# Batch 0's v tails through the SyncE and ScalarE queues with a VectorE cast, and a new order of work

## The chip, the cores and the metric

The kernel runs on one core of a Trainium2 chip. The metric is the device time of one execution in microseconds. The kernel before takes 288.69 us (median of 3 runs, 288.6 to 288.89). The program's span in its profile is 287.0 us.

## The reference

Two blocks follow one another. The first is attention with random features (Performer) over 8 batches of 8 heads, 576 positions, head size 64, 128 features. The second is an MLP mixer over tokens (576 to 256 to 576) and channels (512 to 1536 to 512). Inputs and outputs are fp32.

```python
batch, n_heads, seq, head_dim = (8, 8, 576, 64)
def phi(x):
    proj = np.einsum('bhsd,md->bhsm', x, omega)
    sq = np.sum(x * x, axis=-1, keepdims=True) / 2.0
    h = proj - sq
    h = h - np.max(h, axis=-1, keepdims=True)
    return np.exp(h) / np.sqrt(m)
q_p, k_p = (phi(q_s), phi(k_s))          # q, k times 1 / sqrt(sqrt(64))
kv = np.einsum('bhsm,bhsd->bhmd', k_p, v)
z = np.sum(k_p, axis=2)
num = np.einsum('bhsm,bhmd->bhsd', q_p, kv)
den = np.einsum('bhsm,bhm->bhs', q_p, z)[..., None] + 1e-06
x = num / den                             # then heads side by side: (8, 576, 512)
h = np.maximum(x.T @ w_tok1, 0.0) @ w_tok2     # x.T: per batch, channels by tokens
u = x + h.T
out = u + np.maximum(u @ w_ch1, 0.0) @ w_ch2
```

## The kernel before

**Tiling.** The 576 positions of a batch are 512 "main" positions and a "tail" of 64. Main positions fill 128 partitions four times. The tails of the eight heads are packed together. All matmuls have fp16 operands, so nearly every load casts fp32 to fp16 on its way. Such loads are issued by Pool. The exceptions are batch 0's k (main), which is loaded as fp32 by the SyncE and ScalarE queues into `first_k` and transposed as fp32, and omega.

**Stages of one batch.** Batches 0 and 1 have q and k loaded by position and transposed by TensorE (L485 main, L505 tails). Later batches have them cast to a scratch in DRAM by Pool and transposed by a DMA from the SyncE queue. Then come, for each pair of heads (`hp`): k projection `kp` (L638) and its exp on ScalarE (L514); VectorE's maximum `km` (L664) and its reciprocal (L666); Pool's scaling of v, `vs` (L671); the product `kv` (L684, with the tails' part at L691 or L693); a copy `kvsb` (L701); q projection (L652) and exp; the numerator (L720, L722); and the division into `x` (L729, L730). The tails of k go through one projection per batch (L546, "kt") and exp, the tails of q through L611. The tails of v are loaded by `load_v_tail` into `t_vt` (two loads of four heads each) and spread by Pool into the block-diagonal operand `vbd` (L565 for batch 0 after VectorE's maximum L552, L596 for the others). Every kv product needs `vbd`.

The token mix of batch 0 works by 128 channels (`token_mix_first`: "t1" at L803 and L804, "ut" at L819 and L821); for later batches it is L759, L760 and L776. The channel mix is L854 (first half; L860 and L862 for batch 0's first two blocks) and L892 (second half). The tails of two batches share one token tail (L835), and all tails go through a ninth channel mix at the end. The result is added on VectorE and stored.

**What sets the order.** The program is written down by a planner. Each piece of work is a `Job` with an engine, an assumed cost, a key, dependencies and places (buffers). `Planner.run` steps through assumed time: for the engine that can go first it takes, among the jobs that are ready, the one with the lowest key. The keys of batches 1 and up come from `KEYS` and `NEAR`, those of batch 0 from `HEAD`. For loads the planner keeps an assumed wire time and adds `AFTER`; a product that waits for a load gets an extra margin. Engines then run their instructions in the written order. So assumed costs and keys decide the order, and true times decide the waits. Up to eight loads of a queue are outstanding (`LANES`): the ninth waits for the first.

While batch 0 is under way and TensorE would stand idle by the plan, the planner inserts products on zeros (L943, `warm`). They compute nothing that is used; they end at the first channel mix (L860).

The Pool loads keep the order in which the program lists them (`job.after`). The list before begins:

```python
load_nat_tail(0, "k", -8.7)
load_v_tail(0, -8.65)
load_nat(0, "q", 0, 4, -8.6)
load_v(0, -8.55, (), 0, 4)
load_nat(0, "q", 4, 8, -8.5)
load_nat_tail(0, "q", -8.48)
load_v(0, -8.45, (), 4, 8)
```

then the token weights, the first half of `w_ch1`, and batch 1's k, v tails, q and v.

Of the kernel before, what the change touches and what calls it, by code (L numbers as in the profile page):

```python
# [13 lines left out]
AX = mybir.AxisListType  # L14


KEYS = {"a": -1.349, "as": 0.099, "t": -1.509, "ts": 0.187, "gv": 2.165, "lt": -2.428, "lv": -3.989, "to": -2.341, "tt": 0.635, "ks": 1.094, "km": 0.303, "vs": -0.113, "l1": -0.452, "kt": -0.062}
NEAR = {"1": {"a": -1.734, "as": 0.259, "t": -2.775, "ts": 0.45, "gv": -0.056, "km": -2.03, "vs": -0.397, "kt": 0.253}, "2": {"a": -2.686, "as": 0.0, "t": -0.603, "ts": 0.324, "gv": -1.313, "km": 3.931, "vs": 0.571, "lv": -3.347, "lt": -2.872, "kt": -0.122}}
HEAD = {"kp": [-3.838, -3.822, -3.881, -3.404], "ke": [-2.728, -2.927, -2.827, -2.727], "km": [-4.039, -3.592, -4.221, -2.25], "vs": [-3.448, -3.487, -3.196, -2.472], "qp": [-3.203, -3.403, -3.303, -3.488], "qe": [-3.328, -3.374, -2.153, -3.748], "kv": [-3.407, -3.257, -2.676, -3.133], "ko": [-2.32, -3.035, -3.463, -3.168], "n": [-3.199, -3.47, -3.182, -2.377, -2.999, -3.268, -2.999, -2.899], "no": [-4.124, -3.487, -3.919, -3.144, -3.226, -3.426, -3.126, -2.386], "ktm": -3.643, "kt": -4.584, "kte": -5.022, "qt": -3.759, "qte": -5.587, "kx": [-6.213, -5.658, -5.326, -5.458], "kxo": [-6.855, -7.05, -5.723, -4.783], "ktx": -5.661, "ktxo": -5.912, "qx": [-4.987, -3.488], "qxo": [-4.073, -2.977], "qtx": -4.584, "qtxo": -3.371, "t1": [0.229, -1.008, -0.737, -0.359], "re": [0.072, -0.781, 0.181, -0.024], "ut": [0.056, -0.48, -0.104, -0.341], "uo": [-0.099, -0.259, -0.108, 0.38], "vbd": -8.41, "w1": -9.7, "w1t": -9.38, "w2t": -9.78, "wa": -8.03, "wb": -9.17, "w2": -10.08}
# [18 lines left out]
class Planner:  # L38
# [5 lines left out]
    MARGIN = {"PE": 0.3, "ACT": 0.05, "DVE": 0.05, "POOL": 0.05, "SP": 0.0}  # L44
    LANES = 8
    BEFORE = {"POOL": 1.5, "SP": 0.8, "ACT": 0.8}
    AFTER = 0.8
    SWITCH = 0.1
    COLD = 5.5

# [25 lines left out]
    def run(self):  # L76
# [6 lines left out]
        while any(waiting.values()):  # L83
            choice = None
            for eng, jobs in waiting.items():
                ready = []
                for j in jobs:
                    t = at[eng]
                    ok = True
                    if j.after is not None and j.after.end is None:  # L90
                        continue
                    for d in j.deps:
                        if d.end is None:
                            ok = False
                            break
                        m = self.MARGIN[eng] if d.eng != eng else (-self.LATENCY["PE"] if eng == "PE" else 0.0)
                        if eng == "PE" and self.warm is not None:
                            m = min(m, 0.05)
                        if eng == "PE" and d.wire:
                            m = 0.5  # L100
                        t = max(t, d.end + m)
                    if not ok:
                        continue
                    self.now = t
                    got = []
                    for tag, name in j.take:
# [24 lines left out]
            eng = j.eng  # L131
            waiting[eng].remove(j)
            if self.warm is not None and eng == "PE":
                if j.heavy:
                    self.warm = None
                else:
                    while t - at["PE"] > 0.3:
                        self.now = at["PE"] + 0.1
                        free = [i for i, at_ in enumerate(self.places["bank"]) if at_ < self.now]
                        if free:  # L140
                            i = min(free, key=lambda i: (self.warmed.get(i, 0), i))
                            self.warmed[i] = self.warmed.get(i, 0) + 1
                            self.warm(i)
                            last_rows = False
                        at["PE"] += 0.43 if at["PE"] < self.COLD else 0.22
                    t = max(t, at["PE"])
            self.now = t
            for tag, name in j.take:
                if (tag, name) not in self.held:
                    i = self.find(tag)[0]  # L150
                    self.places[tag][i] = math.inf
                    self.held[tag, name] = i
            cost = j.cost
            if eng == "PE":
                cost += self.SWITCH if j.rows != last_rows else 0.0
                last_rows = j.rows
            at[eng] = t + cost
            if j.wire:
                wire = max(wire, t + cost + self.BEFORE[eng]) + j.wire
                j.end = wire + self.AFTER  # L160
                lanes[eng].append(j.end)
            else:
                j.end = t + cost + self.LATENCY[eng]
            j.start = t
            j.fn()
            for g in j.give:
# [11 lines left out]
def kernel(  # L178
# [12 lines left out]
    nc = tc.nc  # L191

    B, H, S, D = q.shape
# [4 lines left out]
    P = 128  # L198
    SM = 512
# [9 lines left out]
    NPE = 2  # L209
# [15 lines left out]
    place = plan.place  # L225
# [12 lines left out]
    w1t = sb([P, 2, DT], FP16, "w1t")  # L238
    w2 = sb([P, NT, S], FP16, "w2")
# [69 lines left out]
    ld = {}  # L309
# [26 lines left out]
    def load_v_tail(b, key, deps=()):  # L336
        jobs = []
        for g in range(2):
            def tails(g=g):
# [3 lines left out]
                    o = t_vt[place("vt", b)][g * ST : (g + 1) * ST].rearrange("p a (c d) -> p (a c) d", c=2)  # L343
                    i = v[b, :, SM:S, :].rearrange("(a i) t d -> i t a d", i=2)[g]
                nc.gpsimd.dma_start(out=o, in_=i)
# [92 lines left out]
    j_w2 = dma("POOL", HEAD["w2"], 1.7, lambda: nc.gpsimd.dma_start(out=w2, in_=moe_w_tok2.rearrange("(i p) s -> p i s", p=P)))  # L438
    def w2_of(tb, j):
        return w2[:, tb, 0:SM].rearrange("p (c j) -> p j c", j=NJ)[:, j, :]  # L440
    j_wc1 = []
    def load_wc1(i):
        c0 = i * (DC // 2)
        j_wc1.append(dma("POOL", HEAD[("wa", "wb")[i]], (3.9, 4.4)[i], lambda: nc.gpsimd.dma_start(
            out=wc1[:, :, c0 : c0 + DC // 2], in_=moe_w_ch1[:, c0 : c0 + DC // 2].rearrange("(i p) c -> p i c", p=P))))
    load_wc1(0)
    load_nat(1, "k", 0, 8, -9.61)
# [528 lines left out]
```

The softmax here doesn't subtract the row's maximum and nothing guards it: scores larger than these inputs give would overflow.

## Time and profile before

| | before |
|---|---|
| time | 288.69 us |
| span of the profile | 287.0 us |
| PE busy | 280.2 us, 98% |
| PE weight loads busy | 141.6 us, 49% |
| VectorE busy | 152.6 us, 53% |
| ScalarE busy | 153.6 us, 54% |
| Pool busy | 93.7 us, 33% |
| channel mix, L892 and L854 | 100.7 us and 88.7 us of PE |
| Pool's first loads issued | k tails 1.44 us, v tails 2.22 us, q 3.67 us |

PE is TensorE's matmuls, PEld its weight loads, DVE VectorE, ACT ScalarE, SP SyncE. A q after an engine's name is its queue of issued loads. Times in a timeline are microseconds from the start of the span, first the start and then the duration. In brackets stands the idle time of that engine before the instruction, and what ended it. A line of the waits view has the total, the number of times and the longest. Matmuls overlap, so their printed durations are longer than their spacing: a product of 512 columns is printed as 379 ns, and eight of them follow one another in 1.73 us.

### The profile page before, as it was taken

Reading aid. Unit: us, or ns where it says so; the run is one execution under the profiler, and the core shown is the slowest. Engines: PE = TensorE matmul, PEld = TensorE weight load, DVE = VectorE, ACT = ScalarE, POOL = GpSimd, SP = SyncE. Lnnn points to the kernel's source line nnn. Section 1 sums busy time; section 2 is a strip of 40 time slices with the busy share of each in tenths; the row PEclk is TensorE's granted clock in tenths of the full one; section 3 lists DMA queues with packets and bytes.
Section 4 is the critical chain, followed back from the end, with each engine's and each line's share of the span. In section 5 each row is a group of like instructions: output and inputs, shape, how many; then the busy total and the mean of one; then the engine's idle time right before and its main releaser. Section 6 shows DMA issues by size and latency. Waiting matters only on the chain.

```text
span 287.0 us, 5605 instructions
## 1 busy us (share of the span) xinstructions
PE 280.2 (98%) x2186; PEld 141.6 (49%) x2186; DVE 152.6 (53%) x330; ACT 153.6 (54%) x322; POOL 93.7 (33%) x126
## 2 busy tenths in 40 slices
PE   8999999999999999999999999999999999999994
PEld 4585554445544544454445544454455444444442
DVE  3986954546669624745584647564686331031012
ACT  2984872098449552875286537753576402602600
POOL 8994950157015701480166016601141000000000
PEclk9999999999999999999999999999999999999999
DMA  8999999999975995999989967996531042013013
GB/s 191 197 191 195 202 216 143 214 196 190 166 110 149 136 175 117 202 168 198 111 156 206 201 85 144 199 189 95 129 75 39 0 110 110 2 48 116 2 45 102
DMA packets 85721, 39.59 MB, mean 138 GB/s; under 512 B 64384, under 2 KB 80128, under 8 KB 85504
## 3 DMA queue, kind: packets, MB, share of 16 engines
q0 software_dynamic: 34288, 17.45, 44.4%
q1 hardware_dynamic: 50624, 21.01, 33.2%
q10 hardware_dynamic: 784, 0.79, 0.8%
q8 instruction: 17, 0.28, 0.4%
q14 instruction: 8, 0.07, 0.1%
HBM read 35.88 MB, written 16.52 MB: 183 GB/s over the span
## 4 chain that ended last, share of the span: by engine, by line
PE 90%; POOL 5%; DMA 3%; issue 1%; ACT 0%; DVE 0%; POOLq 0%; DVEq 0%
PE bank L892 33%; PE bank L854 32%; PE bank L776 4%; PE bank L759 4%; DMA r<-in_k_dram 3%; PE bank L638 3%; PE bank L652 3%; PE bank L684 2%; PE bank L720 2%; POOL vs L671 1%; PE bank L760 1%; POOL r L313 1%; PE bank L835 1%; PE bank L485 1%; PE bank L722 1%
## 5 line engine op out<-in xcount | busy, mean ns | idle before, releaser
L892 PE MATMUL bank<-wc,r 128*128 128x512 f16 (+2 forms) x444 | 100.7, 374 | 0.0
L874 ACT ACTIVATE r<-bank 128x512 f16<-128x512 f32 x106 | 62.7, 606 | 64.5 <-PE bank L854 64.4
L854 PE MATMUL bank<-uT,wc 128*128 128x512 f16 x376 | 88.7, 379 | 0.0
L892 PEld LDWEIGHTS <-r 128*128 128x128 f16 x444 | 40.9, 98 | 48.9 <-issue 4.4
L854 PEld LDWEIGHTS <-wc 128*128 128x128 f16 x424 | 39.7, 98 | 43.1 <-issue 0.4
L514 ACT ACTIVATE qp<-bank 128x512 f16<-128x512 f32 x64 | 35.8, 646 | 13.0 <-PE bank L652 13.0
L664 DVE TENSOR_REDUCE km<-kp 128x8 f16<-128x1024 f16 x32 | 38.5, 1202 | 2.3 <-ACT kp L514 2.3
L514 ACT ACTIVATE kp<-bank 128x512 f16<-128x512 f32 x64 | 34.6, 630 | 6.6 <-PE bank L638 6.4
L671 POOL TENSOR_TENSOR vs<-v,vs 128x512 f16<-128x512 f16 x32 | 33.3, 1063 | 13.8 <-DVE vs L666 4.3
L901 DVE TENSOR_TENSOR o<-u,bank 128x512 f32<-128x512 f16 x28 | 19.1, 683 | 34.5 <-PE bank L892 34.4
L730 DVE TENSOR_TENSOR x<-bank,rc 128x320 f16<-128x320 f32 x62 | 30.5, 492 | 2.1
L779 DVE TENSOR_TENSOR u<-x,bank 128x512 f16<-128x512 f16 x28 | 17.4, 683 | 9.5 <-PE bank L776 9.5
L729 DVE RECIPROCAL rc<-bank 128x5 f32<-128x5 f32 x62 | 11.5, 186 | 16.0 <-PE bank L722 15.8
L596 POOL TENSOR_TENSOR vbd<-vt,vbd 128x512 f16<-128x512 f16 (+1 forms) x7 | 8.2, 1173 | 35.0 <-PE bank L835 14.8
L380 POOL COPY junk<-kT 128x1 f16<-128x1 f16 x6 | 1.1, 186 | 50.5 <-DMA kT<-k 50.5
L767 DVE TENSOR_SCALAR r<-bank 128x512 f16<-128x512 f32 x7 | 4.8, 692 | 21.1 <-PE bank L760 21.1
L759 PE MATMUL bank<-x,w1m 128*128 128x512 f16 x56 | 14.4, 379 | 0.0
L720 PEld LDWEIGHTS <-qp 128*128 128x128 f16 x256 | 12.3, 98 | 4.0
L684 PEld LDWEIGHTS <-kp 128*128 128x128 f16 x256 | 11.1, 98 | 5.7 <-issue 1.1
L684 PE MATMUL bank<-vs,kp 128*128 128x65 f16 x256 | 12.9, 194 | 0.7 <-ACT r L874 0.7
L720 PE MATMUL bank<-kvsb,qp 128*128 128x65 f16 x256 | 13.5, 194 | 0.0
L776 PE MATMUL bank<-r,w 128*128 128x512 f16 x56 | 13.4, 380 | 0.0
(109 smaller groups left out, 269.5 us busy)
## 6 DMA issues: line engine op xcount, KB each, us to landing
out_dram<-o SPq DMA_DIRECT2D x32, 256.0 KB, 2.7
q<-in_q_dram POOLq DMA_DIRECT2D x6, 576.0 KB, 6.8
wc<-in_moe_w_ch_dram POOLq DMA_DIRECT2D x4, 768.0 KB, 10.6
k<-in_k_dram POOLq DMA_DIRECT2D x6, 512.0 KB, 9.1
v<-in_v_dram POOLq DMA_DIRECT2D x6, 512.0 KB, 6.7
r<-in_q_dram POOLq DMA_DIRECT2D x4, 256.0 KB, 7.2
v<-in_v_dram POOLq DMA_DIRECT2D x4, 256.0 KB, 7.1
out_dram<-o SPq DMA_DIRECT2D x5, 128.0 KB, 2.3
```

The source lines that it names most:

```text
L514: nc.scalar.activation(out=out, in_=in_, func=AF.Exp, bias=0.0, scale=1.0)
L664: nc.vector.reduce_max(out=mx, in_=kpv, axis=AX.X)
L671: nc.gpsimd.tensor_tensor(out=vs[:, :, 0:D], in0=t_v[place("v", b)][:, hh[0] : hh[0] + 2, :].rearrange("p h (j d) -> p (h j) d", d=D), in1 ...
L684: nc.tensor.matmul(ps[:, i, :], kpv[:, 2 * i + j // 2, j % 2, :], vs[:, i * NJ + j, 0 : D + 1], start=(i == 0 and j == 0), stop=False, ski ...
L720: nc.tensor.matmul(ps[:, k, j * 65 : (j + 1) * 65], st, s[:, i, 0 : D + 1], start=True, stop=True)
L730: nc.vector.tensor_tensor(out=t_x[place("x", b)][:, :, (2 * hp + hs[0]) * D : (2 * hp + hs[0] + n) * D].rearrange("p j (i d) -> p i j d", ...
L759: nc.tensor.matmul(ps, w1m[:, j, tb * P : (tb + 1) * P], x[:, j, :], start=(j == 0), stop=False)
L776: nc.tensor.matmul(ps, w2_of(tb, j), r1[:, tb, :], start=(tb == 0), stop=(tb == NT - 1))
L854: nc.tensor.matmul(ps, wc1[:, db, cb * P : (cb + 1) * P], moving(db), start=(db == 0), stop=(db == ND - 1))
L874: nc.scalar.activation(out=o, in_=bank(n), func=AF.Relu)
L892: nc.tensor.matmul(ps[:, cols], r3[:, cb, j * P : (j + 1) * P], wc2[:, cb, cols], start=(cb == 0), stop=(cb == NCB - 1))
L901: nc.vector.tensor_tensor(out=t_o[place("o", (c, j))][:, cols], in0=uu[:, cols], in1=bank(n)[:, cols], op=ALU.add)
```

## The change

Batch 0's two v tail loads no longer go through Pool. The SyncE and ScalarE queues load them as fp32, one each, behind their loads of k, into a part of an output tile that is free at that time (`t_o[0]`). VectorE casts them into `t_vt`. Pool's first load of q then follows directly on the k tails. This is meant to have q under way sooner.

Since the pieces of work have changed, the order has been searched anew: nearly all keys in `KEYS`, `NEAR` and `HEAD` have new values, and some assumed costs were revised (tails of later batches, `w2`, the second half of `w_ch1`, `AFTER`, and the margin of a product that waits for a load). These numbers do nothing at run time but decide the order.

```diff
-    AFTER = 0.8
+    AFTER = 0.9
...
                         if eng == "PE" and d.wire:
-                            m = 0.5
+                            m = 0.2
...
-        ld[w + "t", b] = dma("POOL", key, 0.4, go, deps, cost=0.6)
+        ld[w + "t", b] = dma("POOL", key, 0.5 if b else 0.4, go, deps, cost=0.6)
...
-            jobs.append(dma("POOL", key + 0.01 * g, 0.22 if b < NPE else 0.4, tails, take=[("vt", b)], deps=deps, cost=0.7))
+            jobs.append(dma("POOL", key + 0.01 * g, 0.4 if b else 0.22, tails, take=[("vt", b)], deps=deps, cost=0.7))
...
     load_nat_tail(0, "k", -8.7)
-    load_v_tail(0, -8.65)
+
+    vt32 = t_o[0][:, 0 : 2 * P].rearrange("p (g e) -> p g e", g=2)
+    j_vt32 = []
+    for g in range(2):
+        def first_tails(g=g):
+            (nc.sync, nc.scalar)[g].dma_start(out=vt32[:, g, :], in_=v[0, 4 * g : 4 * g + 4, SM:S, :].rearrange("h (r e) d -> h r (e d)", e=2))
+        j_vt32.append(dma(("SP", "ACT")[g], -9.6, 0.15, first_tails, cost=0.47))
+    ld["vt", 0] = add("DVE", 0.35, HEAD["vtc"], lambda: nc.vector.tensor_copy(out=t_vt[place("vt", 0)], in_=vt32), deps=j_vt32, take=[("vt", 0)])
     load_nat(0, "q", 0, 4, -8.6)
...
-    j_w2 = dma("POOL", HEAD["w2"], 1.7, lambda: ...
+    j_w2 = dma("POOL", HEAD["w2"], 2.1, lambda: ...
...
-        j_wc1.append(dma("POOL", HEAD[("wa", "wb")[i]], (3.9, 4.4)[i], ...
+        j_wc1.append(dma("POOL", HEAD[("wa", "wb")[i]], (3.9, 3.7)[i], ...
```

What the new keys make of the order, as it stands in the built program:

- Pool: k tails, then q's first half and the rest of the loads without the two v tails; the first half of `w_ch1` and batch 1's k are issued before any of Pool's computing; then `vs`, `vbd`, two `vs`, batch 1's k tails, the last `vs`. In batch 1: the loads for batch 2 up to k, the first v tail of batch 2, `vs`, the second v tail, `vs`, `vbd`, `vs`, `vs`. Before, it was `vbd`, both v tails, four `vs`.
- VectorE, batch 0: `km`, the new cast, q, `km`, `km`, the tails' maximum L552, `km`, q. Before, L552 came second.
- TensorE, batch 0: 29 filler products instead of 23, of which ten stand in a row before the first kv product; three kv products in a row; L505 of batch 1 one "ut" block earlier, before the last two. Batch 1: two blocks of four L652 stand before the first kv product instead of after it, and three kv products follow one another.

More of the change, by code (lines that the diff above doesn't have):

```diff
@@ L14 @@
 AX = mybir.AxisListType
-KEYS = {"a": -1.349, "as": 0.099, "t": -1.509, "ts": 0.187, "gv": 2.165, "lt": -2.428, "lv": -3.989, "to": -2.341, "tt": 0.635, "ks": 1.094, "km": 0.303, "vs": -0.113, "l1": -0.452, "kt": -0.062}
-NEAR = {"1": {"a": -1.734, "as": 0.259, "t": -2.775, "ts": 0.45, "gv": -0.056, "km": -2.03, "vs": -0.397, "kt": 0.253}, "2": {"a": -2.686, "as": 0.0, "t": -0.603, "ts": 0.324, "gv": -1.313, "km": 3.931, "vs": 0.571, "lv": -3.347, "lt": -2.872, "kt": -0.122}}
-HEAD = {"kp": [-3.838, -3.822, -3.881, -3.404], "ke": [-2.728, -2.927, -2.827, -2.727], "km": [-4.039, -3.592, -4.221, -2.25], "vs": [-3.448, -3.487, -3.196, -2.472], "qp": [-3.203, -3.403, -3.303, -3.488], "qe": [-3.328, -3.374, -2.153, -3.748], "kv": [-3.407, -3.257, -2.676, -3.133], "ko": [-2.32, -3.035, -3.463, -3.168], "n": [-3.199, -3.47, -3.182, -2.377, -2.999, -3.268, -2.999, -2.899], "no": [-4.124, -3.487, -3.919, -3.144, -3.226, -3.426, -3.126, -2.386], "ktm": -3.643, "kt": -4.584, "kte": -5.022, "qt": -3.759, "qte": -5.587, "kx": [-6.213, -5.658, -5.326, -5.458], "kxo": [-6.855, -7.05, -5.723, -4.783], "ktx": -5.661, "ktxo": -5.912, "qx": [-4.987, -3.488], "qxo": [-4.073, -2.977], "qtx": -4.584, "qtxo": -3.371, "t1": [0.229, -1.008, -0.737, -0.359], "re": [0.072, -0.781, 0.181, -0.024], "ut": [0.056, -0.48, -0.104, -0.341], "uo": [-0.099, -0.259, -0.108, 0.38], "vbd": -8.41, "w1": -9.7, "w1t": -9.38, "w2t": -9.78, "wa": -8.03, "wb": -9.17, "w2": -10.08}
@@ new lines @@
+KEYS = {"a": -1.338, "as": 0.106, "t": -1.828, "ts": 0.0, "gv": 1.889, "lt": -1.751, "lv": -4.321, "to": -2.557, "tt": 0.639, "ks": 0.361, "km": -0.26, "vs": -0.181, "l1": -0.452, "kt": 0.234}
+NEAR = {"1": {"a": -1.419, "as": 0.259, "t": -2.698, "ts": 0.391, "gv": -2.392, "km": -2.03, "vs": -0.455, "kt": 1.511}, "2": {"a": -2.686, "as": 0.0, "t": -0.709, "ts": 0.31, "gv": -0.268, "km": 4.269, "vs": 0.788, "lv": -3.347, "lt": -2.945, "kt": -0.072}}
+HEAD = {"vtc": -4.219, "kp": [-3.838, -3.862, -3.881, -3.404], "ke": [-1.193, -2.927, -2.827, -2.727], "km": [-4.541, -3.927, -4.366, -2.25], "vs": [-3.448, -3.715, -3.196, -2.472], "qp": [-2.901, -3.403, -1.964, -3.488], "qe": [-3.328, -3.374, -2.153, -3.748], "kv": [-2.895, -3.257, -2.676, -3.133], "ko": [-2.32, -3.035, -3.463, -3.596], "n": [-3.199, -3.47, -3.182, -2.377, -2.961, -2.921, -2.999, -2.899], "no": [-4.124, -3.487, -3.919, -3.144, -3.226, -3.426, -3.126, -2.386], "ktm": -2.963, "kt": -4.584, "kte": -5.097, "qt": -3.55, "qte": -5.587, "kx": [-6.213, -5.658, -5.326, -5.458], "kxo": [-6.855, -6.998, -5.723, -4.833], "ktx": -5.111, "ktxo": -5.912, "qx": [-4.987, -3.488], "qxo": [-4.073, -1.402], "qtx": -4.584, "qtxo": -3.595, "t1": [0.229, -1.008, -0.737, -0.359], "re": [0.072, -0.918, 0.181, -0.024], "ut": [0.056, -0.087, -0.104, -0.258], "uo": [-0.099, -0.259, -0.108, 0.38], "vbd": -8.89, "w1": -8.48, "w1t": -9.38, "w2t": -9.16, "wa": -9.24, "wb": -8.68, "w2": -9.03}
@@ L437 @@
     load_w1t(0, HEAD["w1t"])
-    j_w2 = dma("POOL", HEAD["w2"], 1.7, lambda: nc.gpsimd.dma_start(out=w2, in_=moe_w_tok2.rearrange("(i p) s -> p i s", p=P)))
+    j_w2 = dma("POOL", HEAD["w2"], 2.1, lambda: nc.gpsimd.dma_start(out=w2, in_=moe_w_tok2.rearrange("(i p) s -> p i s", p=P)))
     def w2_of(tb, j):
@@ L443, in load_wc1 @@
         c0 = i * (DC // 2)
-        j_wc1.append(dma("POOL", HEAD[("wa", "wb")[i]], (3.9, 4.4)[i], lambda: nc.gpsimd.dma_start(
+        j_wc1.append(dma("POOL", HEAD[("wa", "wb")[i]], (3.9, 3.7)[i], lambda: nc.gpsimd.dma_start(
             out=wc1[:, :, c0 : c0 + DC // 2], in_=moe_w_ch1[:, c0 : c0 + DC // 2].rearrange("(i p) c -> p i c", p=P))))
```

## The prediction

> **What bounds the kernel now.** I read the page's busy shares first, then the waits of the PE, then the timelines of PE and Pool around each wait, and last the landings of loads.
>
> ```profile
> PE 280.2 (98%) x2186; PEld 141.6 (49%) x2186; DVE 152.6 (53%) x330; ACT 153.6 (54%) x322; POOL 93.7 (33%) x126
> ...
> PE   8999999999999999999999999999999999999994
> POOL 8994950157015701480166016601141000000000
> DMA  8999999999975995999989967996531042013013
> ```
>
> TensorE (PE) is the bound: 98% busy, with a dent in the first slices and at the end. What can change is therefore the start, before the steady stretch, and the few waits in it.
>
> ```profile
> PE bank L943 <- DVE mask L423: 1.2, 1, 1.2
> PE bank L684 <- ACT r L874: 0.7, 1, 0.7
> PE bank L505 <- DMA r<-in_k_dram: 0.6, 1, 0.6
> PE bank L611 <- ACT qT L509: 0.2, 1, 0.2
> ```
>
> Two of these matter: 0.6 us at 23.3 (L505, the transposes of batch 1's k tails, wait for their load) and 0.67 us at 35.9 (L684, the first kv product of batch 1). No wait stands after 48 us. The matmuls of L943 are fillers on zeros, so a busy PE before 24 us is not all work.
>
> ```profile
> 23.52 0.75 POOL L331 DMA_DIRECT2D v<-in_v_dram  x1 [1.87 <-DMA r<-in_k_dram]
> 24.25 0.75 POOL L313 DMA_DIRECT2D r<-in_q_dram  x1
> 24.99 0.76 POOL L331 DMA_DIRECT2D v<-in_v_dram  x1
> 25.72 0.85 POOL L459 DMA_DIRECT2D wc<-in_moe_w_ch_dram  x1
> 28.44 0.82 POOL L459 DMA_DIRECT2D wc<-in_moe_w_ch_dram  x1 [1.87 <-issue]
> ...
> 31.70 0.55 POOL L358 DMA_DIRECT2D k<-in_k_dram  x1 [0.22 <-issue]
> 32.27 1.94 POOL L596 TENSOR_TENSOR vbd<-vt,vbd 128x1024 f16<-128x1024 f16 x1
> 34.14 1.30 POOL L345 DMA_DIRECT2D vt<-in_v_dram  x2
> 35.45 3.09 POOL L671 TENSOR_TENSOR vs<-v,vs 128x512 f16<-128x512 f16 x3
> ```
>
> Pool's first vs of batch 1 runs from 35.45 to 36.52; L684 starts at 36.57. So the wait named after ACT is one on Pool. The line at 23.52 shows a second thing: a Pool load goes only when the load eight places before it has landed. There v waits for batch 1's k; it starts 0.29 us after that landing. Pool is thus tied to the stream of loads.
>
> **What the Trainium skill says.** "DMA: Bandwidth & Descriptors", section "Issuing engines are not separate DMA queues": loads from SP, ACT and Pool share the same 16 engines, so another queue saves issue time and no bandwidth. The trace agrees: with Pool's queue backlogged, 194 to 202 GB/s flow from 12 to 36 us, whatever Pool is doing. The same page's specifications put the line rate at pieces of 512 B and more. Here the v tails are written by Pool as pieces of 256 B. The window from 5 to 7 us shows it, 40 slices of 0.05 us:
>
> ```profile
> GB/s 369 348 328 369 328 349 272 272 216 221 191 171 172 172 120 125 196 155 155 156 111 77 73 99 68 104 107 127 140 175 231 164 164 210 205 205 174 184 205 236
> ```
>
> The rate falls to 68 to 127 GB/s while the v tails pass, and returns to about 200 with q's first half. "TensorEngine Tiling (Array Packing)", "Key Properties", says that a change of tiling mode drains TensorE. The trace prices it: 4 matmuls of 512 columns take 0.86 us after their own kind and 0.97 us after a K=64 product, so about 0.1 us a change.
>
> **The change, part by part.**
>
> *The v tails.* Pool's two issues at L345, 1.45 us, go. SP and ACT issue one load each after their k loads; an ACT issue takes 0.48 us, and its table load (1.77 to 3.05) moves to about 2.25 to 3.5, before ACT's first work at 5.51: free. VectorE gets one cast of 128x256 from fp32. The trace has 0.16 us for a 128x128 cast from SBUF and 0.58 to 0.69 for 512 elements from PSUM; "VectorE: DVE Perf Modes", the perf-mode tier table, has 2x for such copies. I take 0.25 us (0.16 to 0.35). It sits between two waits of a VectorE that is busy from 6 to 21 us, so it delays batch 0's x by that much.
>
> *What issuing q sooner is worth.* Pool's queue is full from 5 us on, so what counts is the stream and not the issue. In the stream the two v tails cost 64 KB at 195 GB/s, 0.33 us, plus what the dip loses, about 80 GB/s less than 195 for 1.1 us, 0.45 us: 0.8 us. They come back as 128 KB of fp32 at the 330 to 370 GB/s of the first k loads, 0.4 us. Net, every later load lands 0.4 us sooner (0.1 to 0.8).
>
> *Batch 0.* In the new order VectorE's kt_nb (L552) comes fifth instead of second, so no kv product of batch 0 can run before Pool's vbd and second vs, about 15 us instead of 12.43, and the PE does ten fillers there. Afterwards its work is contiguous, so little is lost. VectorE's sum of work before the last x grows only by the cast, so the last t1 product comes at about 22.3 and L505 at about 23. L505 now stands one "ut" block (L819 and L821, 0.82 us) earlier in the PE's order and waits for the k tails, which land at 23.82 - 0.4 = 23.4. From there to L860: L505 0.22, L485 0.46, two ut 1.64, L638 0.55, L485 0.55, L546 0.22 = 3.64 us, so L860 at about 27.05 against 26.83 before.
>
> *Batch 1, the decisive part.* The new Pool order is: load of k for batch 2, first v tail of batch 2, vs, second v tail, vs, vbd, vs, vs. The first v tail waits for the second half of batch 1's q (eight loads before it), issued at 24.25 and landed 8.6 us later:
>
> ```profile
> r<-in_q_dram POOLq DMA_DIRECT2D x1, 256.0 KB, 8.6
> ```
>
> Before, vbd ran during this wait; now Pool idles. Then: landing 32.8 - 0.4 = 32.4, reaction 0.29, v tail 0.68, vs 1.03, v tail 0.65, vs 1.02, vbd 1.90, vs 1.05 = 39.0. The PE's third kv product needs that last vs: 39.1. The PE is there sooner: 27.05, plus the 9.07 us that lay between L860 and the wait before (26.83 to 35.90), plus two blocks of L652 that now stand in front (0.43 each, with four mode changes of 0.1: 1.27), plus two kv products of 0.36 = 38.1. It waits about 1.0 us for Pool (partly at the first kv, whose vbd ends at 38.0). Three later instructions of the same kv stage are queued behind it, and on ACT and VectorE the copies of kv.
>
> *The sum.* Before, the third kv product started at 38.79; now at 39.1: +0.3. What the PE still has to do from there: counted in the two instruction orders, four more L854 (+0.86), four fewer L652 (-0.43), 56 instead of 60 mode changes (-0.4): about zero. The rest of the matmuls are the same. So 288.69 + 0.3 = **289.0 us**. Both waits of before are gone by name, and a new one on Pool takes what they gave.
>
> *The remaining keys* move kv products, fillers and Pool's vbd of the later batches. There before shows no PE wait; Pool has idle gaps of 4 to 14 us in them, ACT and VectorE are half busy. I cost them at nothing.
>
> **Rivals.**
>
> *A, main:* the Pool wait of batch 1 binds, 289.0. For it: Pool's chain is a sum of durations in the trace. The load's landing is its only loose term: 0.8 sooner gives 288.6, 0.1 sooner 289.3.
>
> *B, faster:* the waits of 0.6 and 0.67 us vanish and nothing replaces them: 288.69 - 1.3 = 287.4, with half of it left 288.0. For it: the two waits are real, and the planner's load costs were redone. Against it: it needs batch 1's second q half to land at 31, 1.8 us sooner, from a stream that is full.
>
> *C, slower:* as A, and the reordered later batches open waits of their own, for instance where vbd now stands before the casts of the next batch: +0.5 to +1.2 on A, 289.5 to 290.2, say 289.8. For it: all orders changed. Against it: the slack on Pool.
>
> *D, slower:* batch 0's kv products at 15 us push the start back: L860 must be later than 28.0 before it, not Pool, sets the third kv. If it comes at 28.6, the end moves 0.6 beyond A: 289.6. For it: VectorE has no gap from 6 to 21 us. Against it: over 1 us of room.
>
> **How the numbers follow.** A 0.50, B 0.13, C 0.24, D 0.13. The bounds of 0.2% are 288.1 and 289.3. A lies within them but for 0.08 on the slow side; C gives 0.05 to "same" and 0.19 to slower; D 0.03 and 0.10. Faster 0.13, same 0.42 + 0.08 = 0.50, slower 0.08 + 0.29 = 0.37. The range runs from 288.2, half of B's gain on a good A, to 289.9, the middle of C: about 2 in 10 lie outside.
>
> **What would show it.** Right: the PE's waits of after name L684 or L693 at 37 to 39 us for 0.8 to 1.3 us in sum, with Pool's vbd and vs ending just before; L505 still waits for its load, near 23.4; Pool idles near 32 until q's second half lands; fillers pile up before 15 us. Wrong: that q half landing before 31.5; the third kv of batch 1 starting before 38.5; L860 after 28; or a PE wait past 48 us.

## The result and the profile after

| | before | after |
|---|---|---|
| time, median of 4 runs | 288.64 us | 290.46 us |
| ratio, 95% interval | | 1.0061 [1.0043, 1.0079] |
| span of the profile | 287.0 us | 288.8 us |
| batch 0: q's first half issued / landed | 3.67 / 8.52 | 2.21 / 10.95 |
| batch 0: v's first half landed | 9.79 | 12.37 |
| batch 0: first kv product (L684, now L691) | 12.43 | 17.70 |
| L860 (now L867) | 26.83 | 30.03 |
| batch 1: third kv product | 38.79 | 41.15 |
| last matmul | 282.68 | 284.85 |

The change made the kernel slower by 0.6%. Lines behind L417 have moved down by 7. The page of the changed kernel, busy times and slices:

```profile
PE 281.5 (97%) x2192; PEld 142.0 (49%) x2192; DVE 153.7 (53%) x331; ACT 153.7 (53%) x322; POOL 91.8 (32%) x124
...
PE   8799999999999999999999999999999999999994
POOL 8498780119112811282108311730142000000000
DMA  7999999799969996969998949799761034102014
```

TensorE is still the bound. Its waits over the whole span (total, times, longest):

```profile
PE bank L492 <- DMA wc<-in_k_dram: 1.2, 1, 1.2
PE bank L950 <- DVE mask L430: 1.2, 1, 1.2
PE bank L492 <- DMA r<-in_q_dram: 0.7, 1, 0.7
```

Both waits of before that the forecast spoke of are gone, and no wait on Pool stands in their place. The new waits are both on loads of batch 0, k and q. The steady stretch is much as before: from the third kv product of batch 1 to the last matmul lie 243.70 us (243.88 before), and behind the last matmul 3.97 (4.31). So +2.36 - 0.18 - 0.34 = +1.84 us, the difference of the spans. All of the loss is made before 41 us.

The stretch from 5 to 7 us, in 40 slices, where before the v tails' dip stood:

```profile
DMA  9899999999999384593699997599799999999799
GB/s 287 266 328 307 328 246 236 216 145 145 144 61 92 41 123 72 102 123 61 113 143 123 154 143 113 102 133 143 123 215 123 195 154 164 195 154 143 113 205 205
```

The dip has not gone: the rate lies at 41 to 154 from 5.5 to 6.4 us, and the DMA engines are at times idle (digits 3 to 5). The runs without v tails, below, show a dip too. The stretch from 5.5 to 11 us by queue (packets, MB, busy time as a share of 16 engines; packets overlap in the record, so a share can be over 100%), first before, then after:

```profile
q0 software_dynamic: 2909, 0.99, 144.6%
q1 hardware_dynamic: 12, 0.01, 0.5%
```

```profile
q0 software_dynamic: 1532, 0.77, 113.7%
q1 hardware_dynamic: 173, 0.10, 8.2%
q10 hardware_dynamic: 132, 0.07, 4.2%
```

q0 is Pool's queue, q1 that of SP, q10 that of ACT. Before, the hardware queues were all but done at 5.5 and Pool's moved 0.99 MB; now they still hold the v tails, and Pool's moves 0.77 MB. The tails' packets run from 5.97 to 9.85 us on ACT's queue and from 6.90 to 10.87 on SP's: four microseconds each for 64 KB. Pool's timeline shows what hangs on the landings:

```profile
8.07 0.72 POOL L445 DMA_DIRECT2D w<-in_moe_w_tok_dram  x1 [1.12 <-DMA r<-in_k_dram]
11.24 0.76 POOL L451 DMA_DIRECT2D wc<-in_moe_w_ch_dram  x1 [2.45 <-DMA r<-in_q_dram]
12.65 0.88 POOL L313 DMA_DIRECT2D r<-in_k_dram  x1 [0.66 <-DMA v<-in_v_dram]
13.55 1.07 POOL L678 TENSOR_TENSOR vs<-v,vs 128x512 f16<-128x512 f16 x1
14.56 0.26 POOL L569 COPY vbd<-mask 128x16 f16<-128x16 f16 x1
14.72 1.88 POOL L572 TENSOR_TENSOR vbd<-vt,mask 128x1024 f16<-128x1024 f16 x1
16.57 2.06 POOL L678 TENSOR_TENSOR vs<-v,vs 128x512 f16<-128x512 f16 x2
```

In the new order three issues, each tied to a landing eight places before it, stand ahead of Pool's first product. They wait 4.2 us in sum, and the kv products come at 17.70.

### The profile page after: what moved, and what is told of

Same layout as the page of the kernel before. It is cut to its first block, busy times and chain, and to the rows that moved or that the text cites. A ratio compares the mean times of both kernels' runs of the same rounds, so it can differ in the third digit from the quotient of the medians.

```text
span 288.8 us, 5603 instructions
## 1 busy us (share of the span) xinstructions
PE 281.5 (97%) x2192; PEld 142.0 (49%) x2192; DVE 153.7 (53%) x331; ACT 153.7 (53%) x322; POOL 91.8 (32%) x124
## 3 DMA queue, kind: packets, MB, share of 16 engines
HBM read 35.88 MB, written 16.52 MB: 181 GB/s over the span
## 4 chain that ended last, share of the span: by engine, by line
PE 85%; DMA 6%; POOL 4%; ACT 2%; DVE 1%; issue 0%; SPq 0%; DVEq 0%
PE bank L899 33%; PE bank L861 30%; PE bank L783 4%; PE bank L766 4%; DMA o<-in_v_dram 3%; DMA r<-in_q_dram 3%; PE bank L659 2%; PE bank L727 2%; PE bank L691 2%; PE bank L645 2%; POOL vs L678 1%; PE bank L767 1%; ACT r L881 1%; PE bank L842 1%; ACT qp L521 1%; POOL vbd L572 1%
## 5 line engine op out<-in xcount | busy, mean ns | idle before, releaser
L861 PE MATMUL bank<-uT,wc 128*128 128x512 f16 x376 | 87.7, 379 | 0.0
L727 PEld LDWEIGHTS <-qp 128*128 128x128 f16 x256 | 11.5, 98 | 3.5 <-issue 0.2
L727 PE MATMUL bank<-kvsb,qp 128*128 128x65 f16 x256 | 12.3, 193 | 0.0
L908 DVE TENSOR_TENSOR o<-ut,bank 128x512 f32<-128x512 f16 (+2 forms) x5 | 2.9, 581 | 17.5 <-PE bank L899 17.4
L691 PEld LDWEIGHTS <-kp 128*128 128x128 f16 x256 | 10.7, 97 | 3.0 <-issue 0.5
L645 PE MATMUL bank<-omT,kT 64*128 64x128 f16 x256 | 12.0, 219 | 0.0
```

The lines of the kernel that those rows point to most:

```text
L645: nc.tensor.matmul(ps[e][:, c : c + M], m[half[e], r, :], omT[half[e]], start=True, stop=True)
L727: nc.tensor.matmul(ps[:, k, j * 65 : (j + 1) * 65], st, s[:, i, 0 : D + 1], start=True, stop=True)
L861: nc.tensor.matmul(ps, wc1[:, db, cb * P : (cb + 1) * P], moving(db), start=(db == 0), stop=(db == ND - 1))
L908: nc.vector.tensor_tensor(out=t_o[place("o", (c, j))][:, cols], in0=uu[:, cols], in1=bank(n)[:, cols], op=ALU.add)
```

## The experiments

Three theories at the start. **1:** the fp32 tails on the hardware queues hold up the whole stream. **2:** q issued sooner crowds out k(6:8), the last quarter (heads 6 and 7) of batch 0's k (it landed at 8.37 in place of 6.84). **3:** the new order is to blame, with the first half of `w_ch1` (the "expert weights" of the expectations) and batch 1's k issued ahead of Pool's products.

Times are medians; each ratio is against the kernel before in the same rounds (288.8 to 289.2 us there, so ratios compare better than times). "q" is the landing of the first half of batch 0's q, "kv" the first kv product of batch 0, "L860" that block's start, "kv3" the third kv product of batch 1, all from one profiled execution. That execution is not always typical: in `old_order_tails_behind_k` it took 292.43 us, the longest of 9, in `same_bytes_512_rows` 290.03, the longest of 21, in `one_piece_128_rows` 289.69, the second longest of 22, in `one_piece_124_rows` 289.47, the second shortest of 9. The changed kernel gave q at 10.95 and at 10.30, so differences of some tenths in these columns say little.

| run | q | kv | L860 | kv3 | time | ratio, 95% |
|---|---|---|---|---|---|---|
| before | 8.52 | 12.43 | 26.83 | 38.79 | 288.64 | 1 |
| after | 10.95 | 17.70 | 30.03 | 41.15 | 290.46 | 1.0061 [1.0043, 1.0079] |
| tails_back_on_pool | 8.41 | 15.49 | 27.57 | 39.31 | 289.37 | 1.0006 [0.9990, 1.0021] |
| no_v_tails | 8.21 | 15.30 | 27.38 | 39.14 | 288.95 | 0.9991 [0.9981, 1.0001] |
| old_order_tails_behind_k | 11.29 | 16.37 | 29.76 | 41.71 | 290.97 | 1.0064 [1.0042, 1.0085] |
| weights_behind_products | 9.99 | 17.23 | 29.60 | 41.23 | 290.97 | 1.0059 [1.0039, 1.0079] |
| tails_ahead_of_k | 9.95 | 17.18 | 31.11 | 43.44 | 293.79 | 1.0165 [1.0150, 1.0180] |
| old_order_no_v_tails | 8.45 | 13.09 | 27.14 | 39.33 | 290.86 | 1.0059 [1.0037, 1.0080] |
| half_the_tails | 9.34 | 14.20 | 28.11 | 39.81 | 291.46 | 1.0086 [1.0069, 1.0104] |
| tails_behind_v_on_pool | 8.44 | 13.95 | 29.03 | 40.96 | 291.36 | 1.0077 [1.0065, 1.0090] |
| tails_by_head | 9.05 | 18.63 | 30.71 | 42.43 | 291.14 | 1.0074 [1.0061, 1.0087] |
| same_bytes_512_rows | 9.41 | 16.52 | 28.59 | 40.08 | 289.27 | 1.0006 [0.9999, 1.0012] |
| same_bytes_1024_rows | 8.76 | 15.50 | 27.73 | 39.71 | 289.17 | 1.0002 [0.9994, 1.0011] |
| old_order_no_v_tails_2 | 8.65 | 13.30 | 27.04 | 38.76 | 289.64 | 1.0022 [1.0010, 1.0034] |
| one_piece_124_rows | 9.70 | 16.36 | 28.72 | 40.03 | 289.73 | 1.0042 [1.0023, 1.0061] |
| one_piece_128_rows | 9.21 | 16.40 | 28.47 | 40.25 | 289.08 | 1.0005 [0.9995, 1.0015] |
| tails_rows_first_2 | 9.35 | 18.60 | 30.68 | 41.59 | 291.39 | 1.0063 [1.0032, 1.0094] |
| rows_first_cast_by_pool | 8.39 | 15.63 | 28.00 | 39.33 | 289.63 | 1.0026 [1.0016, 1.0036] |
| changed_again | 10.30 | 16.96 | 29.33 | 40.86 | 290.42 | 1.0051 [1.0037, 1.0065] |

### Which part of the change costs

`tails_back_on_pool`: the order of after, the tails loaded by Pool.

```diff
+            if (b, w) == (0, "k"):
+                for g in range(2):
+                    nc.gpsimd.dma_start(out=t_vt[0][:, g, :], in_=v[0, 4 * g : 4 * g + 4, SM:S, :]...)
...
-            (nc.sync, nc.scalar)[g].dma_start(out=vt32[:, g, :], ...)
+            pass
```

> The order of the changed kernel, but batch 0's v tails are loaded by Pool again, right behind the k tails, and there is no cast. Theory 1 (the fp32 tails on the sync and ScalarE queues run against Pool's backlog and hold all loads up): k(6:8) lands near 6.9 us as before (8.4 in the changed kernel), q's first half near 8.5, v's near 9.8, batch 0's first kv product comes at 14.5 to 15.5 us, the time 288.4 to 289.2 us. Theory 2 (sooner issue of q alone crowds k's last quarter out): q is issued as late as before here, so the same recovery as theory 1. Theory 3 (Pool issues the expert weights and batch 1's k ahead of its batch 0 products, wherever the tails are loaded): the landings recover but the time stays at 290.0 us or more.

`no_v_tails`: the hardware loads replaced by `pass`, the cast by `nc.vector.memset(t_vt[place("vt", 0)], 0.0)`.

> The changed kernel without batch 0's v tails: their tile is set to zero by VectorE in place of the cast, so that part of the values of batch 0 is left out of the computation. q is still issued at 2.2 us. Theory 1: k(6:8) near 6.9 us, q's first half at or before 8.5 us, the time 288.2 to 288.9. Theory 2: k(6:8) still lands past 7.7 us and q's first half past 9.5, the time 289.8 or more. Theory 3: landings recover, the time 289.8 or more.

`old_order_tails_behind_k`: the kernel before, with the tail loads behind k's on the two queues.

```diff
+            for g in range(2):
+                if h0 == (6, 4)[g]:
+                    (nc.sync, nc.scalar)[g].dma_start(out=vt32[:, g, :], in_=v[0, 4 * g : 4 * g + 4, SM:S, :]...)
...
                     nc.vector.reciprocal(out=vs[:, :, D], in_=mx)
+                if (b, hp) == (0, 0):
+                    nc.vector.tensor_copy(out=t_vt[place("vt", 0)], in_=vt32)
```

> The order of the kernel before, with batch 0's v tails in fp32 on the sync and ScalarE queues behind the four loads of k, and cast by VectorE behind the first reciprocal. Theories 1 and 2: k(6:8) lands past 7.7 us, q's first half past 10.3, batch 0's first kv product at 14 us or later, the time 289.6 to 290.6. Theory 3: with the old order of Pool the delay is taken up, the time is 288.4 to 289.1.

`weights_behind_products`: after, `wc1`'s first half and batch 1's k issued at the end of `vbd` of batch 0.

> The changed kernel with two of Pool's issues moved: the first half of the expert weights and batch 1's k are issued behind batch 0's block of tail values instead of ahead of Pool's first product. Their landings should stay within 0.5 us (21.7 and 24.4), since Pool's queue still has work until 18 us. Theory 3: Pool's first product starts at 12.4 us instead of 13.55, batch 0's first kv product comes at 16.5 instead of 17.7, and the time falls by about 1.1, to 289.3. Theory 1 and 2 alone: the late landings still set batch 0, the time falls by less than 0.4 us.

Three of the four agree. With the tails off the hardware queues q lands at 8.2 to 8.4 and the loss is gone in the new order; with them on, q lands at 10 to 11.3 and the loss is there in the old order too. Theory 3 falls: when the loads come as before, the new order loses nothing that the time can tell (1.0006, up to 1.0021), though kv3 is 0.5 us later than in the kernel before. Theory 2 falls by `no_v_tails`, where q is issued at 2.22 and k(6:8) lands at 6.39. In `old_order_tails_behind_k` k(6:8) lands at 6.46 and q only at 11.29, against what theories 1 and 2 both expected of k; so the late k of after's profile is not the cause either. That run's chain of waits says what is (start, us, what):

```profile
1.44 0.78 POOL r L324
2.22 9.06 DMA r<-in_q_dram
11.29 0.04 issue
11.33 1.03 PE bank L491 x8
```

One load of q, nine microseconds under way, then TensorE. `weights_behind_products` does not decide: the two issues (1.7 us) now stand between `vbd` and the second product, so kv gained only 0.5 us, and the time did not fall.

### What the purpose is worth

`old_order_no_v_tails`: as `old_order_tails_behind_k`, the loads replaced by `pass` and the cast by a memset. `old_order_no_v_tails_2`: the memset moved to the start.

> The order of the kernel before without the loads of batch 0's v tails (tile set to zero by VectorE, so that part of batch 0's values is left out): the ceiling of what issuing q sooner can bring in the old order. q's first half at about 8.2, v's at 9.5, batch 0's first kv product at 12.3. My theory: nothing of these 0.3 us reaches the end beyond 0.3, the time 288.8 to 289.2 against 289.1. The purpose of the change read as a theory (the end follows q): below 288.6.

> The run old_order_no_v_tails again, with the tile of v tails set to zero at the start: there its clearing stood behind the first reciprocal and so held Pool's block of tail values back from 9.08 to about 9.9 us. Now Pool's stream should stand as in the kernel before (weights issued near 12.1, first kv product at 12.4 or sooner). The ceiling of issuing q sooner in the old order: if it is worth nothing, 288.9 to 289.3 against 289.1; if the end follows q, 288.6 or less; if the old order suffers by itself from loads that come sooner, 289.8 or more again.

`tails_behind_v_on_pool`: the kernel before, with `load_v_tail(0, ...)`'s two loads issued behind v's first half.

> The kernel before with batch 0's v tails still loaded by Pool as fp16, but behind v's first half in place of ahead of q: q is issued 1.45 us sooner with no load on another queue and no cast. q's first half at about 8.1, v's at 9.4, the tails at 9.9 to 10.1 (7.3 before), so the block of tail values starts near 10.1 in place of 9.1, batch 0's first kv product at 13.3 to 13.6 (12.4 before). My theory: the end is indifferent to both, 288.8 to 289.3 against 289.1. If the end follows q's landing: below 288.7; if it follows the first kv product: 289.8 or more.

Issuing q at 2.2 in place of 3.67 brings its landing to 8.2 to 8.65, from 8.52: at most 0.3 us, even with the tails left out. Nor does the dip belong to the tails alone, as the forecast had read it. The stretch from 5 to 7 us of `no_v_tails`:

```profile
DMA  9999999999996988998999999999999999999999
GB/s 369 328 348 307 369 287 287 267 267 165 145 195 103 154 123 123 184 113 103 164 133 143 133 143 184 164 184 184 174 205 174 184 174 195 205 205 195 154 225 205
```

The mean rate from 5.5 to 6.5 us is 153 GB/s there, 124 and 141 in the two runs without tails in the old order, 135 in the kernel before, 116 after. So leaving the tails out does not give the dip back. The time is not better in any of these runs; the best is `no_v_tails`, 0.09% with an interval that reaches 1. The old order does worse than I expected: with Pool's tails only moved (`tails_behind_v_on_pool`) it loses 2.2 us. There Pool comes to `vbd` at 10.82 (9.08 before), since two of its issues ahead of it wait for landings:

```profile
8.99 0.54 POOL L440 DMA_DIRECT2D w1t<-in_moe_w_tok_dram  x1 [1.09 <-DVE kT L496]
10.11 0.72 POOL L442 DMA_DIRECT2D w<-in_moe_w_tok_dram  x1 [0.58 <-DMA v<-in_v_dram]
```

In Pool's order of issues, eight places before them stand q's first half, landed at 8.44, and v's, landed at 9.82 (the profile puts the first wait down to VectorE). So the `w_ch1` weights go out at 13.85 (12.10 before), batch 1's k tails land at 26.0 (23.82), and L860 follows. In the first run of the pair part of the loss (0.9 us on Pool) was my placing of the memset. What the second still loses, 0.2%, lies behind kv3 (38.76): in its profile the stretch from there to the last matmul is 0.4 us longer, and the one behind the last matmul 0.8 us, for the last stores land 3.0 us after their issue, in place of 2.0.

### Why the tails hold Pool's stream up

`tails_ahead_of_k`: as `old_order_tails_behind_k`, with `(2, 0)[g]` in place of `(6, 4)[g]`.

> The order of the kernel before, the fp32 v tails on the sync and ScalarE queues ahead of k's third and fourth loads, so that they move while Pool's queue is still empty. If the tails' 512-byte rows are slow by themselves (few DMA engines carry each load), each takes over 1.5 us here too and k(6:8) lands past 7.5. If they are slow only against Pool's backlog, both are down in about 0.5 us (128 KB at the 330 KB/us that the two queues reached), k(6:8) lands at about 7.0 to 7.3, q's first half at 8.3 to 8.8, batch 0's first kv product comes at 12.6 to 13.5, the time 288.6 to 289.2 against 289.1 of the kernel before on this chip. A gain would need the end to follow q: below 288.4.

`half_the_tails`: only the SP half on a hardware queue, the other half by Pool behind v's first half.

> As the run with the old order and the tails behind k, but only the sync queue's half of the tails is loaded there; the other half is loaded by Pool behind v's first half. If the delay comes from the amount of hardware-queue packets left against Pool's backlog, it halves: q's first half lands at about 9.7 (8.2 with none, 11.3 with both), the time 289.6 to 290.2. If one queue is enough to hold an engine up, q's first half lands past 10.5 again and the time stays near 290.9.

The stretch from 4.5 to 6 us of `tails_ahead_of_k`:

```profile
DMA  3332431111120218233374527979735649634555
GB/s 82 96 96 55 109 82 41 41 41 55 41 55 27 68 55 123 41 55 55 96 137 109 96 96 150 164 164 191 137 96 123 177 82 205 191 96 137 137 177 164
```

This was the turn. Without any backlog of Pool's, the DMA engines stand mostly idle, at 27 to 123 GB/s in the first half of this stretch, while ACT's tails pass (3.66 to 6.04 us); in before, under k's loads, the mean rate from 4.5 to 5 us is 369. So the tails are slow by themselves, and what queues behind them (k here, landed at 8.92 and 9.12) suffers. Half of them costs q 0.9 us (9.34, against 8.45 with none and 11.29 with both), a third of the whole where half was expected, and the time stays high.

`tails_by_head`: each tail load cut into four, one head each. `same_bytes_512_rows` and `same_bytes_1024_rows`: 64 KB in one piece in place of each tail load.

```diff
-            ...dma_start(out=vt32[:, g, :], in_=v[0, 4 * g : 4 * g + 4, SM:S, :].rearrange("h (r e) d -> h r (e d)", e=2))
+            ...dma_start(out=vt32[:, g, :], in_=v[0, g, 0 : 2 * P, :].rearrange("(r e) d -> r (e d)", e=2))
```

> The changed kernel with each of the two hardware loads of batch 0's v tails cut into four, one for each head (32 partitions of 512 bytes, a source without the jump between heads). If the jump in the source makes the transfer slow, the 128 KB are down before 6.5 us, q's first half lands at about 8.4 (10.0 to 10.95 in the changed kernel), the first kv product comes at 15.3 and the time falls to 289.0 to 289.5 against 289.1 of the kernel before. If it is the length of the rows or the amount, nothing changes: q's first half past 9.9, the time 290.5 to 291.0. The four issues of ScalarE could also run into its first work at 5.35 us.

> The changed kernel in which each hardware load reads 64 KB in one piece, 128 rows of 512 bytes of v's first rows, in place of the tails of four heads (so the values of batch 0's tails are left out: other values stand in their place). Same bytes, rows and partitions as the tails; only the source has no jump. Jump as the cause: the load is down before 6.5 us and q's first half lands at 8.4. Row length or amount as the cause: past 9.9, like the changed kernel.

> The changed kernel in which each hardware load reads 64 KB in one piece as 64 rows of 1024 bytes, the row length of k's loads (the values of batch 0's tails are left out: others stand in their place). If the row length is the cause: down before 6.5 us, q's first half at 8.4, while the run with 512-byte rows stays past 9.9. If the amount alone is the cause: past 9.5 in all. If the jump is the cause: 8.4 in both runs of the same bytes.

The same bytes in the same rows, in one piece, cost 0.06% in place of 0.6%: the form of the source matters, not the amount or the queue. Cutting by head was no cure, and the miss has at least one reason of its own, on ScalarE:

```profile
1.75 3.98 ACTq L419 DMA_DIRECT2D o<-in_v_dram  x4
5.76 1.28 ACT L498 ACT_TABLE_LOAD   x1 [5.76 <-DMA wc<-in_k_dram]
7.06 0.59 ACT L498 CAST kT<-bank 128x512 f16<-128x512 f32 x1
```

Four issues took 3.98 us, and ScalarE's first cast of k came at 7.06 (5.35 in after). SyncE's four loads moved until 11.8 us.

Then I counted packets. Each load ends with packets of 4 bytes, one for each DMA engine that carries it:

```
completion packets of 4 bytes for each v tail load (SP, ACT)      first..last packet: ACT's load    SP's load
after                      4, 4                                   5.97 .. 9.85                      6.90 .. 10.87
old_order_tails_behind_k   4, 4                                   5.86 .. 9.66                      6.20 .. 10.65
one_piece_124_rows         4, 4                                   4.40 .. 6.60                      6.61 .. 8.77
one_piece_128_rows         16, 16                                 5.30 .. 7.08                      5.54 .. 7.52
rows_first_cast_by_pool    16, 16                                 5.23 .. 6.64                      5.39 .. 6.67
each load of k, in all of them: 16
```

The Trainium skill, "DMA: Bandwidth & Descriptors", section "Why a DMA increments its semaphore by 16 and not by 1", says that a hardware-queue load uses the largest number of engines, up to 16, that divides the slowest dimension of both its patterns, and that only these engines post a completion. The slowest dimension of the tails' source is the four heads: 4. The count agrees. Two kinds of kernel follow: one piece of 124 = 4 x 31 rows, and the tails with their 32 rows outermost.

```diff
+    vt32 = sb([32, 4, 2, P], FP32, "vt32")
...
+            ...dma_start(out=vt32[:, :, g, :], in_=v[0, 4 * g : 4 * g + 4, SM:S, :].rearrange("h (r e) d -> r h (e d)", e=2))
...
+    [nc.vector.tensor_copy(out=t_vt[place("vt", 0)][32 * i : 32 * i + 32], in_=vt32[:, i]) for i in range(4)]
```

> As same_bytes_512_rows (64 KB a load in one piece, rows of 512 bytes, no jump; other values stand in place of the v tails), but 124 rows in place of 128, so 3% fewer bytes. If the number of engines is the cause and 124 rows go to 4 engines where 128 go to 16, each load ends with 4 completion packets, q's first half lands past 9.9 us and the time is 290.3 to 291.0, like the changed kernel. If the jump between heads is the cause, nothing changes: q's first half near 9.4, the time 289.1 to 289.4.

> same_bytes_512_rows again, beside the run with 124 rows on the same chip: 16 completion packets a load, q's first half near 9.4 us, 289.1 to 289.4 us.

> The changed kernel, its whole computation, with each tail load laid out with its 32 rows first and the four heads inside: 32 partitions of four pieces of 512 bytes, the jump between heads stays. VectorE moves them to their places by four casts of 32 partitions, some 0.8 us more than the one cast. Engines as the cause: 16 completion packets a load, q's first half at 8.6 to 9.4 us, first kv product at 15.5 to 17, the time 289.0 to 289.9 (the casts may cost part of it). Jump as the cause: 9.9 or later, 290.5 or more. In neither case do I expect less than the 289.1 of the kernel before: without any tails it was the same within 0.2%.

> tails_rows_first again with the tails in a tile of their own: there they lay over columns of the expert weights' first half, so the casts waited for that load and read its values. The whole computation. Landings as in that run (tails by 7.8 us, q's first half 8.6 to 9.1). Four casts of about 0.3 us on VectorE (1.2 us in all) in place of one of 0.26 delay batch 0's remaining VectorE work by some 0.9 us: first kv product at 16.2 to 16.8 (15.3 without tails, 17.7 in the changed kernel), L860 at about 28.3 (30.03), the time 289.2 to 289.8 against 288.9 of the kernel before. If the jump or the mere presence of the tails on these queues were the cause: 290.3 or more.

124 rows post 4 completions and lose 0.42%, 128 rows post 16 and lose nothing that can be told, 3% more bytes included. The two loads together take 4.4 us with 4 completions and 2.2 with 16; in after they take 4.9. Taken at its middle the loss with 124 rows is some two thirds of that of after, and less than expected: 289.73 us in place of 290.3 or more, q at 9.70 and not past 9.9. The two profiles don't show the difference (kv3 at 40.03 with 124 rows and 40.25 with 128): they are of a short and of a long execution, so the times alone bear it. The run with 124 rows also clears `t_vt` on VectorE at the start (0.17 us at 1.11); TensorE's first filler comes at 1.19 in both. The rest may be a late start: with the heads outermost ACT's issue takes 1.16 us, in place of 0.62 with 124 rows, and its first packet comes 1.6 us later. With the rows outermost the jump between heads stays, yet the load has 16 completions and an issue of 0.49 us. The issues between 1.7 and 2.4 us, with KB and us to landing, of after (the profile gives no landing for the loads with 4 completions), then of `rows_first_cast_by_pool`:

```profile
r<-in_q_dram POOLq DMA_DIRECT2D x1, 256.0 KB, 8.7
r<-in_k_dram POOLq DMA_DIRECT2D x1, 64.0 KB, 6.4
o<-in_v_dram ACTq DMA_DIRECT2D x1, 64.0 KB
o<-in_v_dram SPq DMA_DIRECT2D x1, 64.0 KB
```

```profile
r<-in_q_dram POOLq DMA_DIRECT2D x1, 256.0 KB, 6.2
r<-in_k_dram POOLq DMA_DIRECT2D x1, 64.0 KB, 5.7
vt<-in_v_dram ACTq DMA_DIRECT2D x1, 64.0 KB, 5.6
vt<-in_v_dram SPq DMA_DIRECT2D x1, 64.0 KB, 5.4
```

`tails_rows_first` had the tails over columns of the first half of `w_ch1`; its four casts waited 10.4 us for that load and took its values for the tails, so only its landings count (q 8.74; its time was 301.28). `tails_rows_first_2` had q back at 9.35 and lost the gain on VectorE, whose four casts took 2.67 us (told at the end); its 11 executions spread from 288.62 to 292.63 us. `rows_first_cast_by_pool` gives the casts to Pool while it waits for landings:

> As tails_rows_first_2, the whole computation, but the four casts are done by Pool just ahead of its issue of the expert weights, where it waits for landings from 8.6 to 9.6 us; VectorE has no cast. In tails_rows_first_2 the casts stood against Pool's first product (one of them took 1.81 us beside it in place of 0.29) and held VectorE up by 2.4 us. If the form of the tail loads was the whole loss: q's first half at 8.7 to 9.4, first kv product at 15.3 to 16.5, L860 at 27.4 to 28.6, 288.8 to 289.5 against 289.0 of the kernel before. If something else in the change costs time: 290 or more.

> The changed kernel once more, on the same chip as the repaired one: 290.3 to 291.0; 4 completion packets for each tail load, q's first half at 10 to 11.3 us.

Pool's timeline there:

```profile
8.12 1.73 POOL L451 CAST vt<-vt 32x256 f16<-32x256 f32 x4
9.80 0.76 POOL L451 DMA_DIRECT2D wc<-in_moe_w_ch_dram  x1
10.56 0.89 POOL L313 DMA_DIRECT2D r<-in_k_dram  x1
11.51 1.06 POOL L678 TENSOR_TENSOR vs<-v,vs 128x512 f16<-128x512 f16 x1
```

Repaired, the change stands at 1.0026, half-way back from 1.0051 on the same chip. Its first product on Pool starts at 11.51, against 10.74 in `no_v_tails`: the casts cost 0.8 us there; that they are all that is left of the loss is not shown. No version beats the kernel before.

## Why the prediction was wrong

- *"The v tails"*: "SP and ACT issue one load each ... free". ACT's issue took 1.16 us in place of the 0.48 I took, and the table load ran to 4.24; ScalarE's first work stayed at 5.35, so this cost nothing by itself. The cast took 0.29 us, where 0.25 was taken.
- *"What issuing q sooner is worth"*: the step that failed. I let the tails come back "as 128 KB of fp32 at the 330 to 370 GB/s of the first k loads, 0.4 us". They took four microseconds, carried by 4 engines (by the count of completions) and begun late, and Pool's loads came late with them: "every later load lands 0.4 us sooner" became 2.43 later for q's first half, 1.14 for batch 1's k, 1.22 for the second half of batch 1's q. I took a rate measured on loads of another form for these. The gain set against it, 0.8 us of the stream, was misread too: the dip stands without the tails as well, and with them left out q lands at most 0.3 us sooner.
- *"Batch 0"*: kv "about 15 us" was 17.70, L860 "27.05" was 30.03. The order was read rightly: with the loads in time the runs have 15.3 to 15.5 and 27.4 to 27.6. The step left out is Pool's wait for landings ahead of its first product: the new order ties three issues to them.
- *"Batch 1, the decisive part"*: q's second half landed at 34.04 (32.4), the third vs ended at 40.88 (39.0), kv3 came at 41.15 (39.1). From the landing to the end of that vs the sum is 6.84 us, forecast 6.6. `tails_back_on_pool` and `no_v_tails` have kv3 at 39.31 and 39.14. TensorE did not wait, since it came late itself; Pool was done only 0.27 us earlier, so both ways to kv3 were late by the same loads. That these two runs have kv3 where the forecast put it, at 39.1, is luck in part, for the wait is another. In both Pool's third vs ends 0.26 us before kv3, and TensorE waits for VectorE's copy of batch 1's q (L499), ahead of its second block of L652 (there L659); of `no_v_tails`:

```profile
PE bank L659 <- DVE qT L499: 0.7, 1, 0.7
```

- *"The sum"*: what remains behind kv3, "about zero", was -0.18 us. No wait stands past 48 us: C did not happen.
- *Rivals*: D came true by its sign and its mark (L860 after 28), not by its reason, VectorE without a gap, and at twice its size (+1.8 us in place of +0.9). The bound of "0.1 to 0.8" on the sooner landing had no end on the late side.

Open: in the old order with its loads moved the time grows by more than kv3 shows (`half_the_tails` +1.0 us at kv3, +2.3 in time; `old_order_no_v_tails` +0.5 and +1.7). Of that, 0.7 and 0.8 us lie behind the last matmul, where the last stores land 3.0 us after their issue, in place of 2.0; why they do is not known. Open is also how the loss divides between the few engines and the late start. The trace does not name the engine of a packet; that Pool's loads lag on just the engines that carry the tails is inferred from the counts.

## What to carry to other kernels

Before moving a load to another queue, look at the outermost dimension of both its sides: here, in the changed kernel, the loads with four heads outermost posted 4 completions, moved 64 KB in four microseconds each, and Pool's loads behind them landed 1.1 to 2.4 us later. Don't take a rate from loads of another form on the same queue; count the completion packets. Issuing q sooner into a stream that was full brought at most 0.3 us here, and with a limit of eight loads under way, each issue moved forward can be one that waits for a landing.

## What the runs showed of the hardware that was not expected

VectorE's cast from SBUF can take several times as long when a product of Pool falls into it. In `tails_rows_first_2` the four equal casts (min, median, max in ns), and Pool's product at that time:

```profile
L420 DVE CAST vt<-vt x4: 247/284/1809, 10.7 to 13.1; 32x256 f16<-32x256 f32 x4
```

```profile
11.85 1.07 POOL L678 TENSOR_TENSOR vs<-v,vs 128x512 f16<-128x512 f16 x1
12.86 0.33 POOL L569 COPY vbd<-mask 128x16 f16<-128x16 f16 x1
```

The one of 1809 ns runs from 11.27 to 13.08, over the whole of that product, and ends 0.16 us after it. But it began 0.58 us before the product, and the two casts ahead of it took 0.25 and 0.29 us, so the product does not explain all of it. In `tails_by_head` the one cast of 128x256 took 1.00 us beside the same product, ending 0.15 us after it, and 0.29 in after, where Pool was issuing a load. That the product holds the cast is inferred from these two overlaps; no run tested it. VectorE's maximum (1.21 us) was as long beside `vbd` as without it.
